# First batch of an attention-plus-MLP kernel as a stream of score and v rounds, wide relu in two batches, and free instruction order on three engines

## Chip, cores and metric

One NeuronCore of one Trainium2 chip. The metric is the device time of one execution in microseconds (us), lower is better. Times are medians over several runs.

TensorE is called PE below, VectorE DVE, ScalarE ACT, GpSimd POOL, SyncE SP. In the traces PE, ACT, DVE and POOL run side by side, each its own instructions, and one waits where it needs what another has made or still holds: in the kernel before PE waited 17.7 us for DVE between 8 and 52 us.

## The reference

Attention without softmax (relu squared in its place), then a two-layer MLP with relu squared.

```python
def _attn_ref(q, k, v):                       # q, k, v: (8, 12, 448, 64) fp32
    S = q.shape[2]
    scale = 1.0 / np.sqrt(q.shape[-1])
    scores = scale * np.matmul(q, k.transpose(0, 1, 3, 2))
    attn = np.maximum(scores, 0.0) ** 2 / S
    return np.matmul(attn, v).astype(np.float32)

def _moe_ref(x, w_in, w_out):                 # x: (3584, 768); w_in (768, 2048), w_out (2048, 768)
    h = x @ w_in
    r = np.maximum(h, 0.0)
    return ((r * r) @ w_out).astype(np.float32)

def reference(q, k, v, moe_w_in, moe_w_out):
    a = _attn_ref(q, k, v)                    # then (B, S, H * D) rows into the MLP
    ...
```

## The kernel before

A *unit* is four heads of one batch (three units a batch, 24 in all). A unit has seven *rounds*; a round computes one score tile `sp` (128 x 2 x 448 in PSUM) and turns it into `at` (fp16, SBUF) by relu squared. When a unit's seven tiles are there, `av` multiplies them by v into two PSUM tiles, which are evicted as `xt`. When three units of a batch are done, its *dense* work is queued: `hps` (x times w_in, relu squared into `g`) and, a batch later, `ops` (g times w_out, evicted as `osb` and stored). The dense matmuls are fed to PE in slices between score rounds. The first dense matmul can only come after the third unit; until then PE has transposes, scores and av alone, which kept it busy for 29.5 of the first 56.0 us.

```python
ctx.enter_context(tc.manual_schedule())       # all engines run in program order
...
s_p  = ...tile_pool(name="sps", bufs=2, space=PSUM)     # score tiles
mm_p = ...tile_pool(name="mmps", bufs=4, space=PSUM)    # av, hps, ops, transposes

def relu2(ps, dst, scale):                    # ps stays in PSUM through both
    nc.scalar.activation(out=dst, in_=ps, func=AF.Square, scale=scale)          # ACT
    nc.vector.scalar_tensor_tensor(                                             # DVE
        out=dst, in0=ps, scalar=0.0, in1=dst, op0=ALU.is_gt, op1=ALU.mult)

def soft(n, t, sp):
    at = at_p.tile([P, 2, S], FP16, name="at", tag="at")
    relu2(sp[:, :, 0:S], at, SK)
    ats[n, t] = at

def av(n):                                    # 28 matmuls, then two evictions
    ...
    for f in range(2):
        nc.scalar.activation(out=xts[b][:, 2 * u + f, :], in_=ap[f][:, 0:S],
                             func=AF.Copy, scale=CX)
...
for i in range(NB):                           # a burst is two rounds
    g = []
    for r in (2 * i, 2 * i + 1):
        n, t = divmod(r, TJ)
        g.append((n, t, scores(n, t)))        # PE
    if i in avs:
        av(avs[i])                            # PE, then ACT (xt)
    for a in g:
        soft(*a)                              # ACT, DVE
    if i in pushes:
        push_dense(pushes[i])
    upkeep(i)                                 # loads, casts, transposes of later units
    nxt = min([j for j in pushes if j > i] or [NB + 2])
    run_some(max(0.0, (queued - KEEP) / (nxt - i)))     # a slice of dense work
```

## Time and profile before

The kernel before takes 445.16 us (443.25 to 446.56, three runs). Its profiled run has a span of 441.0 us.

I cut the span at three marks of the trace: the first `hps` matmul (dense work can start), the first `ops` matmul (the second batch has been pushed) and the last `hps` matmul.

| stretch, profiled run before | us | what holds it |
|---|---|---|
| start to first hps | 56.0 | chains through ACT and DVE; PE busy 29.5 us |
| first hps to first ops | 45.0 | PE and DVE about even (busy 36.1 and 35.1 us) |
| first ops to last hps | 311.3 | PE (busy 307.2 us) |
| last hps to end | 28.7 | PE (ops; busy 23.8 us), then the last store |

First the page: busy time of each engine, and the row by slices of a fortieth of the span (11 us each) in tenths, with the granted PE clock.

```profile
PE 396.6 (90%) x3092; PEld 202.9 (46%) x3092; DVE 250.3 (57%) x309; ACT 261.8 (59%) x408; POOL 69.6 (16%) x92
...
PE   2565687799999999999999999999999999999995
...
PEclk9996599999999999999999999999999999999999
```

PE is full from the ninth slice on, and short of work in the first eight. In two of these its granted clock was also down, at 0.66 (33 to 44 us) and 0.50 (44 to 55 us).

The next lines are from the queries for one tile, with the start of the first and last instruction of each group: `hps` with the first and last quarter of w_in, and `ops` with the first quarter of w_out. The marks are 56.0, 101.0 and 412.3 us.

```profile
L166 PE MATMUL hps<-xt,w_0_90 x192: 352/353/363, 56.0 to 388.3; 128*128 128x448 f16 x192
...
L166 PE MATMUL hps<-xt,w_3_93 x192: 352/353/363, 88.5 to 412.3; 128*128 128x448 f16 x192
...
L194 PE MATMUL ops<-w_0_94,g x224: 326/326/337, 101.0 to 433.8; 128*128 128x384 f16 x112
```

The waits of PE from 8 to 52 us (who waited <- for whom: us in total, times, longest):

```profile
PE sp L240 <- DVE at L151: 17.7, 17, 3.0
...
```

And the waits of PE from 93 to 400 us, the whole list:

```profile
PE sp L240 <- DVE at L151: 4.5, 9, 0.6
```

PE waits for DVE to be done with a score tile, so that its PSUM can be written again: 17.7 us in 17 waits. In the long later part that is only 4.5 us.

One av burst of the first batch in the timeline (start, duration, engine, line, what; in brackets the engine's idle time before it and who ended it):

```profile
23.97 2.88 PE L263 MATMUL avt<-at,vs 64*64 64x448 f16 x28
...
26.91 0.98 ACT L269 ACTIVATE xt<-avt 128x448 f16<-128x448 f32 x2 [4.44 <-PE avt L263]
...
27.77 1.74 ACT L150 ACTIVATE at<-sp 128x896 f16<-128x896 f32 x2
...
28.73 1.09 DVE L151 SCALAR_TENSOR_TENSOR at<-sp,at 128x896 f16<-128x896 f32 x1 [5.13 <-ACT at L150]
```

ACT is idle for 4.44 us until av is finished, and DVE for 5.13 us.

The same spot in the later part, at the end of a unit:

```profile
120.06 0.57 PE L240 MATMUL sp<-qT,kT 64*64 64x448 f16 x8
...
120.47 1.49 PE L263 MATMUL avt<-at,vs 64*64 64x448 f16 x28
...
122.01 0.98 ACT L269 ACTIVATE xt<-avt 128x448 f16<-128x448 f32 x2 [2.30 <-PE avt L263]
...
122.88 1.74 ACT L150 ACTIVATE at<-sp 128x896 f16<-128x896 f32 x2
123.83 2.09 DVE L151 SCALAR_TENSOR_TENSOR at<-sp,at 128x896 f16<-128x896 f32 x2 [3.96 <-ACT at L150]
...
125.97 0.38 PE L240 MATMUL sp<-qT,kT 64*64 64x448 f16 x4 [0.49 <-DVE at L151]
```

### The profile page before, as it was taken

The numbers are of one execution on the slowest core, as the hardware profiler recorded it, in microseconds if no ns is written. First come the engines' busy times: TensorE is split into PE (matmuls) and PEld (weight loads), VectorE is DVE, ScalarE is ACT, GpSimd is POOL, SyncE is SP. The second block draws the span as 40 slices with busy tenths as digits, with TensorE's granted clock in tenths as the row PEclk, the third lists the DMA queues.
The fourth block names the chain that finished last, engine by engine and source line by source line (L and its number), as shares of the span: only waits on it lengthen the run. The fifth ranks groups of instructions, "written<-read, shape, count | busy, mean of one in ns | idle before, by whom it ended". The sixth has DMA issues, their size and how long they took to land.

```text
span 441.0 us, 7546 instructions
## 1 busy us (share of the span) xinstructions
PE 396.6 (90%) x3092; PEld 202.9 (46%) x3092; DVE 250.3 (57%) x309; ACT 261.8 (59%) x408; POOL 69.6 (16%) x92
## 2 busy tenths in 40 slices
PE   2565687799999999999999999999999999999995
PEld 1232243344445555444445455444445555555563
DVE  2754577776766574676586566486657555222100
ACT  4655478766676576587676665677667656433211
POOL 3710340131003100031103110310110000000000
PEclk9996599999999999999999999999999999999999
DMA  9699899667335764494647462595461111111122
GB/s 244 135 238 211 155 265 177 172 74 158 120 83 120 184 161 79 120 175 91 155 125 114 125 170 57 147 196 83 122 162 36 38 37 36 37 36 37 36 74 72
DMA packets 62883, 53.58 MB, mean 122 GB/s; under 512 B 35712, under 2 KB 59264, under 8 KB 62848
## 3 DMA queue, kind: packets, MB, share of 16 engines
q1 hardware_dynamic: 50944, 41.30, 37.3%
q0 software_dynamic: 11904, 11.80, 17.2%
q8 instruction: 24, 0.39, 0.4%
q14 instruction: 11, 0.09, 0.1%
HBM read 45.61 MB, written 11.01 MB: 128 GB/s over the span
## 4 chain that ended last, share of the span: by engine, by line
PE 76%; DVE 9%; ACT 8%; issue 4%; DMA 1%; SPq 0%; ACTq 0%; DVEq 0%
PE ops L194 31%; PE hps L166 27%; PE sp L240 9%; DVE at L151 9%; PE avt L263 8%; ACT at L150 4%; ACT xt L269 3%; PE tps L103 1%; DMA kf<-in_k_dram 1%; ACT kT L105 0%; DVE g L151 0%; DVE qT L105 0%; ACT ks L89 0%; ACT osb L201 0%; SPq L80 0%
## 5 line engine op out<-in xcount | busy, mean ns | idle before, releaser
L151 DVE SCALAR_TENSOR_TENSOR at<-sp,at 128x896 f16<-128x896 f32 x168 | 175.3, 1086 | 117.5 <-ACT at L150 117.3
L150 ACT ACTIVATE at<-sp 128x896 f16<-128x896 f32 x168 | 147.2, 925 | 27.9 <-PE sp L240 24.3
L194 PEld LDWEIGHTS <-g 128*128 128x128 f16 x896 | 85.3, 98 | 65.2 <-issue 8.9
L151 DVE SCALAR_TENSOR_TENSOR g<-hps,g 128x448 f16<-128x448 f32 x128 | 76.6, 618 | 41.0 <-ACT g L150 40.8
L240 PE MATMUL sp<-qT,kT 64*64 64x448 f16 x672 | 58.9, 392 | 34.0 <-DVE at L151 30.7
L150 ACT ACTIVATE g<-hps 128x448 f16<-128x448 f32 x128 | 68.9, 560 | 29.0 <-PE hps L166 28.5
L201 ACT ACTIVATE osb<-ops 128x384 f32<-128x384 f32 x56 | 27.7, 495 | 53.3 <-PE ops L194 45.6
L269 ACT ACTIVATE xt<-avt 128x448 f16<-128x448 f32 x48 | 23.5, 541 | 58.0 <-PE avt L263 58.0
L240 PEld LDWEIGHTS <-kT 64*64 64x64 f16 x672 | 16.9, 107 | 73.1 <-issue 69.7
L194 PE MATMUL ops<-w_2_96,g 128*128 128x384 f16 x224 | 47.0, 326 | 0.0
L194 PE MATMUL ops<-w_0_94,g 128*128 128x384 f16 x224 | 46.4, 326 | 0.0
L194 PE MATMUL ops<-w_3_97,g 128*128 128x384 f16 x224 | 46.3, 326 | 0.0
L194 PE MATMUL ops<-w_1_95,g 128*128 128x384 f16 x224 | 46.2, 327 | 0.0
L89 POOL CAST qs<-qf 128x896 f16<-128x896 f32 x23 | 21.5, 935 | 152.5 <-DMA qf<-in_q_dram 133.7
L166 PE MATMUL hps<-xt,w_1_91 128*128 128x448 f16 x192 | 40.9, 353 | 0.0
L166 PE MATMUL hps<-xt,w_2_92 128*128 128x448 f16 x192 | 40.7, 353 | 0.0
L166 PE MATMUL hps<-xt,w_3_93 128*128 128x448 f16 x192 | 40.5, 353 | 0.0
L263 PE MATMUL avt<-at,vs 64*64 64x448 f16 x672 | 39.7, 375 | 0.0
L166 PE MATMUL hps<-xt,w_0_90 128*128 128x448 f16 x192 | 39.7, 353 | 0.0
L114 POOL DMA_DIRECT2D vs<-in_v_dram x32 | 20.1, 636 | 94.8 <-PE hps L166 74.9
L263 PEld LDWEIGHTS <-vs 64*64 64x64 f16 x672 | 22.5, 114 | 12.5 <-issue 0.4
L166 PEld LDWEIGHTS <-w_1_91 128*128 128x128 f16 x192 | 18.1, 98 | 19.0 <-issue 4.0
(29 smaller groups left out, 113.0 us busy)
## 6 DMA issues: line engine op xcount, KB each, us to landing
qf<-in_q_dram SPq DMA_DIRECT2D x24, 448.0 KB, 4.5
kf<-in_k_dram SPq DMA_DIRECT2D x24, 448.0 KB, 5.0
out_dram<-osb SPq DMA_DIRECT2D x56, 192.0 KB, 2.7
vs<-in_v_dram POOLq DMA_DIRECT2D x32, 168.0 KB, 5.0
w_0_90<-in_moe_w_in_dram POOLq DMA_DIRECT2D x1, 768.0 KB, 7.4
w_1_91<-in_moe_w_in_dram POOLq DMA_DIRECT2D x1, 768.0 KB, 13.2
w_2_92<-in_moe_w_in_dram POOLq DMA_DIRECT2D x1, 768.0 KB, 17.2
w_3_93<-in_moe_w_in_dram POOLq DMA_DIRECT2D x1, 768.0 KB, 20.4
```

The source lines that it names most:

```text
L89: op(t.rearrange("p t (f d) -> p f t d", f=2), src.rearrange("p f (t d) -> p f t d", d=D))
L103: nc.tensor.transpose(ps[:, t * P:(t + 1) * P], src[:, t, :], ident)
L114: nc.gpsimd.dma_start(out=vst[b][64 * r:64 * r + 64, :, e, :], in_=src[h])
L150: nc.scalar.activation(out=dst, in_=ps, func=AF.Square, scale=scale)
L151: nc.vector.scalar_tensor_tensor(out=dst, in0=ps, scalar=0.0, in1=dst, op0=ALU.is_gt, op1=ALU.mult)
L166: nc.tensor.matmul(cell[0][:, 0:S], lhsT=w1[f // 4][:, m, (f % 4) * P:(f % 4 + 1) * P], rhs=xt[:, m, :], start=(m == 0), stop=(m == NM - 1))
L194: nc.tensor.matmul(cell[0][:, 0:HALF], lhsT=gt[f][:, tb * P:(tb + 1) * P], rhs=w2[f // 4][:, f % 4, hf * HALF:(hf + 1) * HALF], start=(f = ...
L201: nc.scalar.activation(out=cell[1][:, hf * HALF:(hf + 1) * HALF], in_=cell[0][:, 0:HALF], func=AF.Copy, scale=CO)
L240: nc.tensor.matmul(sp[64 * c:64 * c + 64, e, 0:S].rearrange("p (t c) -> p t c", t=TJ), lhsT=kT[r, t, 64 * e:64 * e + 64], rhs=qT[r, :, 64 ...
L263: nc.tensor.matmul(ap[f][64 * e:64 * e + 64, 0:S], lhsT=vs[r, u, e, t * D:(t + 1) * D], rhs=at[r, e, :], start=(t == 0), stop=(t == TJ - 1 ...
L269: nc.scalar.activation(out=xts[b][:, 2 * u + f, :], in_=ap[f][:, 0:S], func=AF.Copy, scale=CX)
```

## The change

Its intent: keep PE fed until dense work can start. The first batch becomes a stream: each round emits one score tile and, three rounds behind it, one v round, so that av no longer comes in bursts. For batches 0 and 1 the relu goes to SBUF as fp32 (ACT), which is meant to free PSUM without waiting for DVE, and the squaring reads SBUF (DVE, one tile of seven on POOL). Some small jobs move: the transposes' copies and, for these two batches, xt to DVE, and the q casts of all six units to ACT. Loads are issued in another order, and small DVE memsets that held some of them back are gone. And only PE and SP keep program order; ACT, DVE and POOL are ordered by the scheduler.

```diff
-    ctx.enter_context(tc.manual_schedule())
+    ctx.enter_context(tc.manual_schedule(engines={mybir.EngineType.PE, mybir.EngineType.SP}))
...
-    osb_p = ctx.enter_context(tc.tile_pool(name="osbp", bufs=3))
+    rel_p = ctx.enter_context(tc.tile_pool(name="widep", bufs=5))     # relu tiles and osb
...
+    def relu2_wide(ps, dst, scale, eng):
+        r = rel_p.tile([P, 2, S], FP32, name="rel", tag="wide")
+        nc.scalar.activation(out=r, in_=ps, func=AF.Relu, scale=scale)
+        eng.tensor_mul(dst, r, r)
...
     def soft(n, t, sp):
-        relu2(sp[:, :, 0:S], at, SK)
+        if n < NPE:                                   # NPE = 6 units, two batches
+            relu2_wide(sp[:, :, 0:S], at, SK, nc.gpsimd if t == 5 else nc.vector)
+        else:
+            relu2(sp[:, :, 0:S], at, SK)
...
-    def av(n):                                        # seven v rounds at once
+    def av(n, t):                                     # one v round; evicts after the seventh
...
+            if n < NPE:
+                nc.vector.tensor_scalar(
+                    out=dst, in0=ap[f][:, 0:S], scalar1=CX, scalar2=None, op0=ALU.mult)
+            else:
+                nc.scalar.activation(out=dst, in_=ap[f][:, 0:S], func=AF.Copy, scale=CX)
...
-    cast_qk(1, "q", pool)
     cast_qk(1, "k", pool)
+    cast_qk(1, "q", act)
...
+    early = {1: [(load_w1, 0)], 2: [(load_w1, 1)], 3: [(load_w1, 2)], 4: [(load_w1, 3)],
+             5: [(load_v, 1, (0, 1))], 7: [(load_v, 1, (2, 3))]}
...
                 if n == 0:
-                    cast_qk(2, "q", pool)
                     cast_qk(2, "k", pool)
+                    cast_qk(2, "q", act)
...
-    for i in range(NB):
+    for r in range(STREAM):                           # STREAM = 21 + LAG, LAG = 3
+        n, t = divmod(r, TJ)
+        sp = scores(n, t)
+        soft(n, t, sp)
+        if r >= LAG:
+            av(*divmod(r - LAG, TJ))
+        if n + 1 < NPE and t in (3, 5):
+            turn_pe(n + 1, "kq"[t // 4], dve)
+        if r % 2 == 0:
+            upkeep(r // 2)
+    push_dense(0)
+
+    for i in range(STREAM // 2, NB):                  # bursts as before, av ahead of soft
...
```

(The diff is cut; comments after code are mine.)

More of the change, by code (lines that the diff above doesn't have):

```diff
@@ L72, with load_qk @@
     vst: dict = {}
-    def load_qk(n, w, gate=None):
+    def load_qk(n, w, eng):
         b, u = divmod(n, NU)
         t = raw_p.tile([P, 2, TJ * D], FP32, name=w + "f", tag=w + "f")
-        if gate is not None:
-            gate.memset(t[:, 0, 0:1], 0.0)
         src = q if w == "q" else k
-        nc.sync.dma_start(
+        eng.dma_start(
             out=t,
@@ L183, in store @@
                     "(p t) d -> p t d", t=TJ)[:, t, :],
-                in_=osb[64 * i:64 * i + 64, :])
+                in_=osb[64 * i:64 * i + 64, 0:DM])
     def o_groups(pr, tb):
@@ L199, in run @@
                     if hf == 0:
-                        cell[1] = osb_p.tile([P, DM], FP32, name="osb", tag="osb")
+                        cell[1] = rel_p.tile([P, 2 * S], FP32, name="osb", tag="wide")
                     nc.scalar.activation(
@@ L247, in soft @@
         at = at_p.tile([P, 2, S], FP16, name="at", tag="at")
-        relu2(sp[:, :, 0:S], at, SK)
+        if n < NPE:
+            relu2_wide(sp[:, :, 0:S], at, SK, nc.gpsimd if t == 5 else nc.vector)
+        else:
+            relu2(sp[:, :, 0:S], at, SK)
         ats[n, t] = at
-    def av(n):
+    avs_open: dict = {}
+    def av(n, t):
         b, u = divmod(n, NU)
-        if u == 0:
+        if n == NU * b and t == 0:
             xts[b] = x_p.tile([P, NM, S], FP16, name="xt", tag="xt")
@@ L255, in av @@
         vs = vst[b]
-        ap = [mm_p.tile([P, 512], FP32, name="avt", tag="mm") for _ in range(2)]
-        for t in range(TJ):
-            at = ats.pop((n, t))
-            for e in range(2):
-                for c in range(2):
-                    f = c ^ e
-                    r = slice(64 * c, 64 * c + 64)
-                    nc.tensor.matmul(
-                        ap[f][64 * e:64 * e + 64, 0:S],
-                        lhsT=vs[r, u, e, t * D:(t + 1) * D],
-                        rhs=at[r, e, :],
-                        start=(t == 0), stop=(t == TJ - 1), skip_group_check=True)
@@ L268, in av @@
-        for f in range(2):
-            nc.scalar.activation(
-                out=xts[b][:, 2 * u + f, :], in_=ap[f][:, 0:S], func=AF.Copy, scale=CX)
-    pool, dve, act = nc.gpsimd.tensor_copy, nc.vector.tensor_copy, nc.scalar.copy
-    for n in range(3):
-        load_qk(n, "q")
-        load_qk(n, "k")
-    load_v(0, (0, 1))
+        if t == 0:
+            avs_open[n] = [mm_p.tile([P, 512], FP32, name="avt", tag="mm") for _ in range(2)]
+        ap = avs_open[n]
+        at = ats.pop((n, t))
@@ new lines, in av @@
+        for e in range(2):
+            for c in range(2):
+                f = c ^ e
+                r = slice(64 * c, 64 * c + 64)
+                nc.tensor.matmul(
+                    ap[f][64 * e:64 * e + 64, 0:S],
+                    lhsT=vs[r, u, e, t * D:(t + 1) * D],
+                    rhs=at[r, e, :],
+                    start=(t == 0), stop=(t == TJ - 1), skip_group_check=True)
+        if t < TJ - 1:
+            return
+        for f in range(2):
+            dst = xts[b][:, 2 * u + f, :]
+            if n < NPE:
[3 more added lines that the diff above has]
+                nc.scalar.activation(out=dst, in_=ap[f][:, 0:S], func=AF.Copy, scale=CX)
@@ L279 @@
+    pool, dve, act = nc.gpsimd.tensor_copy, nc.vector.tensor_copy, nc.scalar.copy
+    NPE = 6
+    load_qk(0, "k", nc.sync)
+    load_qk(0, "q", nc.scalar)
+    for n in (1, 2):
+        load_qk(n, "k", nc.sync)
+        load_qk(n, "q", nc.sync)
     ident = const_p.tile([P, P], FP16, name="ident", tag="ident")
     make_identity(nc, ident)
-    load_v(0, (2, 3))
-    cast_qk(0, "q", dve)
-    cast_qk(0, "k", act)
+    load_v(0, range(4))
+    cast_qk(0, "k", dve)
+    cast_qk(0, "q", act)
+    turn_pe(0, "k", dve)
@@ L284 @@
     turn_pe(0, "q", dve)
-    turn_pe(0, "k", act)
-    cast_qk(1, "q", pool)
     cast_qk(1, "k", pool)
+    cast_qk(1, "q", act)
     KEEP = 4000.0
-    NPE = 6
     ROUNDS = NUN * TJ
     NB = ROUNDS // 2
+    LAG = 3
+    STREAM = NU * TJ + LAG
     def av_burst(n):
         return (TJ * (n + 1) - 1) // 2 + 2
-    pushes = {av_burst(NU * b + 2): b for b in range(B)}
-    avs = {av_burst(n): n for n in range(NUN)}
+    pushes = {av_burst(NU * b + 2): b for b in range(1, B)}
+    avs = {av_burst(n): n for n in range(NU, NUN)}
@@ L300, in upkeep @@
+    early = {1: [(load_w1, 0)], 2: [(load_w1, 1)], 3: [(load_w1, 2)], 4: [(load_w1, 3)],
+             5: [(load_v, 1, (0, 1))], 7: [(load_v, 1, (2, 3))]}
     def upkeep(i):
+        for fn, *a in early.get(i, ()):
+            fn(*a)
         r0 = 2 * i
         for n in range(NUN):
+            b, u = divmod(n, NU)
             if r0 <= TJ * n < r0 + 2:
-                b, u = divmod(n, NU)
-                if 0 < n and n + 2 < NUN and n + 2 >= 3:
-                    load_qk(n + 2, "q", nc.vector if n + 2 < 6 else None)
-                    load_qk(n + 2, "k", nc.vector if n + 2 < 6 else None)
+                if 0 < n and n + 2 < NUN:
+                    for w in "kq":
+                        load_qk(n + 2, w, nc.sync)
@@ L309, in upkeep @@
                 if n == 0:
-                    cast_qk(2, "q", pool)
                     cast_qk(2, "k", pool)
-                    for z in range(4):
-                        load_w1(z)
-                    load_v(1, range(4))
+                    cast_qk(2, "q", act)
                 elif n == 3:
@@ L321, in upkeep @@
                 if 2 < n + 2 < NUN:
-                    cast_qk(n + 2, "q", pool)
                     cast_qk(n + 2, "k", pool)
-                if n + 1 < NUN:
-                    if n + 1 < NPE:
-                        turn_pe(n + 1, "q", dve)
-                        turn_pe(n + 1, "k", act)
+                    cast_qk(n + 2, "q", act if n + 2 < NPE else pool)
+                if STREAM <= r0 and n + 1 < NPE:
+                    for w in "kq":
+                        turn_pe(n + 1, w, dve)
                 if NPE <= n + 2 < NUN:
-                    turn_dma(n + 2, "q")
-                    turn_dma(n + 2, "k")
-    for i in range(NB):
+                    for w in "kq":
+                        turn_dma(n + 2, w)
+    for r in range(STREAM):
[10 more added lines that the diff above has]
+    for i in range(STREAM // 2, NB):
         g = []
@@ L337 @@
         if i in avs:
-            av(avs[i])
+            for t in range(TJ):
+                av(avs[i], t)
         for a in g:
@@ L347 @@
     for j in sorted(j for j in avs if j >= NB):
-        av(avs[j])
+        for t in range(TJ):
+            av(avs[j], t)
     for j in sorted(j for j in pushes if j >= NB):
```

## The prediction

> **What bounds the kernel now.** From about 93 us on it is TensorE. In the table of windows PE is busy 93.5 of 95 us (188 to 283 us), and the waits of PE between 93 and 400 us sum to only 4.5 us. Before that it is not: first dense matmul (hps) at 55.98 us, and from 54 to 93 us PE is busy 30.5 of 39 us. The waits of PE on the DVE half of relu-squared are 17.7 us up to 54 us and 8.5 us from 54 to 93. The timeline shows why. A score tile stays in PSUM through score matmuls (0.6 us), ACT Square (0.93) and DVE (1.09), with two buffers and two rounds per burst: a burst every 2.73 us (11.06, 13.79). Each of the three av bursts adds a hole: PE av 2.9 us, then xt on ACT, then scores again; DVE is idle about 5 us (23.6 to 28.7). The granted clock is 0.50 in much of 32 to 54 us.
>
> **What the change does.** (1) For batches 0 and 1 ACT writes Relu to SBUF and frees PSUM; chain per two rounds 0.6 + 0.93 = 1.6 us. The square costs DVE about what it cost before[...] 1.086 us measured for the PSUM form; no run shows the new form yet. (2) One round in seven goes to POOL[...]. (3) av is spread with a lag of three, removing the av holes. (4) DVE gets both turn copies (0.62 each) and xt (about 0.6 each); ACT gets a q cast (0.94).
>
> **Limit of the stream: DVE.** Per unit 6 x 1.09 + 2 x 0.62 + 2 x 0.6 = 9.0 us, ACT 7.5 us. Three units from 9.6 us would give dense work at about 38 us. [...]ACT may also be held by a q cast whose DMA is late (the second unit's loads landed at 9 to 11.3 us before). First hps: about 41 us, 14 to 15 us earlier.
>
> **Next ten bursts (before: 52 to 90.5 us).** DVE-bound again, estimated 11.7 us a unit plus contention against 12.8 before: gain 0 to 5 us, I take 1.
>
> **On the critical path.** All of this lies ahead of the TensorE-bound stretch, so it goes through to the end. DMA is the second limit: reads needed before dense work are about 13.6 MB, near 36 us at the rate of the saturated stretch, so the start cannot move much below 38 us. Later batches: order of ACT, DVE and POOL now chosen by the scheduler, at most 1% either way.
>
> **Predicted: 430 us, 421 to 440.** Faster by over 2% 0.76, within 2% 0.21, slower 0.03.
>
> **What would show it.** First hps at 38 to 45 us; score waits released by ACT, not DVE; DVE over 80% busy from 10 to 40 us; DVE squares near 1.09 us, longer where POOL overlaps; clock at 0.50 for less time; after the second batch, the same 47.5 us per batch.
>
> **What would make it wrong.** Strong DVE/POOL blocking (squares over 1.4 us on average, first hps past 47 us); weight loads hoisted by the scheduler that delay q and k; ACT blocked early by a cast; a worse order in the steady part.

Three passages are cut from this text, as what they argued rested on no run or trace of this case. The 1.09 us of a wide square: the 1.086 us of the old form, measured in the kernel before, gives the same term. An allowance of 1 us a unit for squares that POOL's work holds up (the "contention" of its paragraph on the ten bursts): estimate, and not shown by the trace of before, where POOL's 46 casts all took 0.93 to 0.94 us. The forecast of about 41 us for the first hps came from the 38 us above it and three times this allowance. The third is an estimate of a POOL square's time; the six of the kernel after took 1.95 us on average. The 430 us are 445.16 less about 14 us at the first hps and 1 us in the ten bursts.

Of the terms, 0.62 is the copy of qT on DVE in the kernel before (617 ns), 0.94 its cast of k on ACT (937 ns), and 0.6 for xt on DVE an estimate, near the 618 ns that DVE took there for `g`, which has the size of xt and also comes from PSUM. Run after the forecast, the kernel after took 0.610 us for xt.

## More of the kernel before

The instructions that stand in line on an engine are called its queue here.

Note the place of `av` and `soft` in a burst: in program order ACT meets the eviction of `av` first and the Square of the two fresh score tiles after it.

## The result, and the profile after

The kernel after takes 429.34 us (427.43 to 429.66, four runs), the one before 444.64 us in the same rounds. The ratio is 0.9646, with a 95% interval of 0.9606 to 0.9686. A ratio here is the mean time of one kernel's fast runs over that of the other's fast runs of the same rounds, so it is not quite the ratio of the medians. Executions over 1.5% slower than the fastest of the same kernel are left out of the means.

The gain in time is the predicted one, 15.3 us against 15.2. Its place is not.

| stretch, profiled runs | before | after | gain | the prediction's term |
|---|---|---|---|---|
| start to first hps | 56.0 | 50.7 | 5.3 | 14 to 15 |
| first hps to first ops | 45.0 | 40.6 | 4.4 | about 1 (its ten bursts are nearly this stretch) |
| first ops to last hps | 311.3 | 305.7 | 5.6 | none ("at most 1% either way", entered as 0) |
| last hps to end | 28.7 | 28.6 | 0.1 | none |
| span | 441.0 | 425.6 | 15.4 | |

The marks after:

```profile
L170 PE MATMUL hps<-xt,w_0_90 x192: 349/352/363, 50.7 to 373.0; 128*128 128x448 f16 x192
...
L170 PE MATMUL hps<-xt,w_3_93 x192: 352/352/363, 77.6 to 397.0; 128*128 128x448 f16 x192
...
L198 PE MATMUL ops<-w_0_94,g x224: 326/326/336, 91.3 to 418.5; 128*128 128x384 f16 x112
```

The same lines of the page (a slice is 10.6 us here):

```profile
PE 389.6 (92%) x3092; PEld 198.4 (47%) x3092; DVE 261.8 (62%) x315; ACT 255.5 (60%) x395; POOL 79.3 (19%) x93
...
PE   2456688799999999999999999999999999999995
...
PEclk9988899999999999999999999999999999999999
```

The PE row is hardly better in the first eight slices. It is not the row of a kernel whose start was cured. The waits of PE from 8 to 52 us:

```profile
PE sp L244 <- ACT rel L155: 8.1, 7, 6.7
PE tps L101 <- DVE xt L284: 5.0, 2, 2.9
PE avt L274 <- DVE at L156: 3.1, 3, 1.3
PE hps L170 <- DVE xt L284: 1.9, 1, 1.9
...
```

Score tiles are now released by ACT, as intended, but new waits have come: 8.1 us for ACT, 6.7 of them at once, and 5.0 and 1.9 us for `mm` PSUM that DVE had not emptied of av. From 93 to 400 us the list of PE's waits is now empty.

The 6.7 us are at the very start:

```profile
8.11 0.96 PE L244 MATMUL sp<-qT,kT 64*64 64x448 f16 x8 [0.72 <-DVE qT L103]
...
9.43 0.94 ACT L87 CAST qs<-qf 128x896 f16<-128x896 f32 x1 [3.15 <-DMA qf<-in_q_dram]
...
13.94 0.94 ACT L87 CAST qs<-qf 128x896 f16<-128x896 f32 x1 [3.57 <-DMA qf<-in_q_dram]
14.78 1.72 ACT L155 ACTIVATE rel<-sp 128x896 f32<-128x896 f32 x2
...
15.74 0.59 PE L244 MATMUL sp<-qT,kT 64*64 64x448 f16 x4 [6.67 <-ACT rel L155]
```

Two score tiles are ready before 9.1 us. But the q casts of the second and third unit stand ahead of the first Relu in ACT's queue (the program puts the first of them there, the scheduler the other as well), and those wait for loads. In the trace ACT stands 3.57 us in front of the second cast with Relus ready behind it. The first Relu starts at 14.78 us; before, the first Square started at 8.97.

The later part, at the same spot as above:

```profile
109.56 0.57 PE L244 MATMUL sp<-qT,kT 64*64 64x448 f16 x8
...
109.96 1.49 PE L274 MATMUL avt<-at,vs 64*64 64x448 f16 x28
110.00 1.73 ACT L148 ACTIVATE at<-sp 128x896 f16<-128x896 f32 x2 [0.72 <-PE sp L244]
...
110.94 2.09 DVE L149 SCALAR_TENSOR_TENSOR at<-sp,at 128x896 f16<-128x896 f32 x2 [1.58 <-ACT at L148]
...
111.61 0.99 ACT L287 ACTIVATE xt<-avt 128x448 f16<-128x448 f32 x2
```

Here is the part that the prediction had not seen. The program text of the bursts still says av first, then relu squared. With ACT free, the scheduler has swapped them: the Squares run *beside* av, and xt comes after. DVE's idle time falls from 3.96 to 1.58 us, and PE never waits for PSUM.

Finally the new squares on DVE, from the page's groups:

```profile
L156 DVE TENSOR_TENSOR at<-rel 128x896 f16<-128x896 f32 x36 | 43.7, 1253 | 11.6 <-ACT rel L155 11.5
```

Their mean is 1253 ns. Undisturbed ones take 1.08 us (those with no POOL work near them), seven of the 36 take 1.7 to 2.5 us, six of them where a POOL cast or square ran beside them and one where POOL was issuing loads. 36 x (1253 - 1080) ns = 6.2 us, on average about 1 us for each of the six units. (In all ten profiled runs with wide squares, none of the 139 squares without any POOL work beside them took over 1.2 us, and 91 of the 160 beside a cast or square did.) The prediction charged 1 us a unit for this, the author's estimate. For this kernel that term was right.

### The profile page after: what moved, and what is told of

Read it like the earlier page. It is cut to its first block, busy times and chain, and to the rows that moved or that the text cites. A ratio compares the mean times of both kernels' runs of the same rounds, so it can differ in the third digit from the quotient of the medians.

```text
span 425.6 us, 7547 instructions
## 1 busy us (share of the span) xinstructions
PE 389.6 (92%) x3092; PEld 198.4 (47%) x3092; DVE 261.8 (62%) x315; ACT 255.5 (60%) x395; POOL 79.3 (19%) x93
## 4 chain that ended last, share of the span: by engine, by line
PE 82%; DVE 10%; DMA 3%; ACT 2%; issue 2%; SPq 0%; ACTq 0%; DVEq 0%
PE ops L198 35%; PE hps L170 32%; PE sp L244 8%; DVE at L156 7%; PE avt L274 6%; DMA qf<-in_q_dram 3%; ACT rel L155 1%; DVE g L149 1%; PE tps L101 1%; DVE xt L284 1%; SPq L78 0%; DVE qT L103 0%; DVE at L149 0%; DVE kT L103 0%; ACT qs L87 0%
## 5 line engine op out<-in xcount | busy, mean ns | idle before, releaser
L149 DVE SCALAR_TENSOR_TENSOR at<-sp,at 128x896 f16<-128x896 f32 x126 | 131.6, 1086 | 66.0 <-ACT at L148 65.8
L148 ACT ACTIVATE at<-sp 128x896 f16<-128x896 f32 x126 | 108.8, 915 | 40.9 <-PE sp L244 40.5
L149 DVE SCALAR_TENSOR_TENSOR g<-hps,g 128x448 f16<-128x448 f32 x128 | 77.5, 620 | 53.0 <-ACT g L148 52.3
L244 PE MATMUL sp<-qT,kT 64*64 64x448 f16 x672 | 53.5, 379 | 13.1 <-ACT rel L155 8.1
L87 POOL CAST ks<-kf 128x896 f16<-128x896 f32 x23 | 23.1, 1003 | 197.0 <-DMA kf<-in_k_dram 185.8
L156 DVE TENSOR_TENSOR at<-rel 128x896 f16<-128x896 f32 x36 | 43.7, 1253 | 11.6 <-ACT rel L155 11.5
L274 PE MATMUL avt<-at,vs 64*64 64x448 f16 x672 | 41.7, 364 | 3.1 <-DVE at L156 3.1
L155 ACT ACTIVATE rel<-sp 128x896 f32<-128x896 f32 x42 | 35.8, 920 | 12.8 <-PE sp L244 12.8
L244 PEld LDWEIGHTS <-kT 64*64 64x64 f16 x672 | 15.4, 107 | 45.8 <-issue 40.3
L274 PEld LDWEIGHTS <-vs 64*64 64x64 f16 x672 | 21.3, 110 | 15.4 <-issue 5.5
```

Source lines behind the costliest of these rows:

```text
L87: op(t.rearrange("p t (f d) -> p f t d", f=2), src.rearrange("p f (t d) -> p f t d", d=D))
L149: nc.vector.scalar_tensor_tensor(out=dst, in0=ps, scalar=0.0, in1=dst, op0=ALU.is_gt, op1=ALU.mult)
L155: nc.scalar.activation(out=r, in_=ps, func=AF.Relu, scale=scale)
L156: eng.tensor_mul(dst, r, r)
L244: nc.tensor.matmul(sp[64 * c:64 * c + 64, e, 0:S].rearrange("p (t c) -> p t c", t=TJ), lhsT=kT[r, t, 64 * e:64 * e + 64], rhs=qT[r, :, 64 ...
L274: nc.tensor.matmul(ap[f][64 * e:64 * e + 64, 0:S], lhsT=vs[r, u, e, t * D:(t + 1) * D], rhs=at[r, e, :], start=(t == 0), stop=(t == TJ - 1 ...
```

## The experiments

My theory after the result, in three parts:

- **A (order).** The gain behind the first hps comes from ACT squaring the scores ahead of evicting xt, not from the stream or the wide form. Rival R: the first batches leave the later ones in a better state.
- **B (lost start).** The stream's own gain was cut by ACT's late start (casts ahead of the first Relu) and by PE waiting for PSUM that DVE empties late. Rival: loads, or DVE with POOL, bound it anyway.
- **C (parts).** What the wide form, the POOL squares and the spread av are worth each.

All twelve experiments gave correct results. They ran in four groups, each with its own runs of the kernel before, so between groups compare ratios. The time of a profiled run differs from the median of its kernel by up to 3 us (before: 442.76 us, against medians of 444.64 to 445.85), so stretches read from one profile carry that; the stretch from first ops to last hps is an exception and repeats within 0.1 us.

| run | median us | ratio to before (95%) | first Relu or Square | start to first hps | first hps to first ops | first ops to last hps |
|---|---|---|---|---|---|---|
| before | 444.64 | 1 | 8.97 | 56.0 | 45.0 | 311.3 |
| after | 429.34 | 0.9646 (0.9606 to 0.9686) | 14.78 | 50.7 | 40.6 | 305.7 |
| b_free | 433.36 | 0.9727 (0.9698 to 0.9757) | 8.79 | 58.6 | 39.6 | 305.7 |
| b_soft | 427.41 | 0.9599 (0.9574 to 0.9624) | 9.36 | 51.2 | 39.6 | 305.7 |
| a_man | 434.95 | 0.9775 (0.9751 to 0.9799) | 10.35 | 49.2 | 44.0 | 311.3 |
| a_man_soft | 427.10 | 0.9613 (0.9586 to 0.9641) | 10.19 | 49.1 | 43.5 | 305.7 |
| a_qpool | 427.10 | 0.9578 (0.9550 to 0.9607) | 8.86 | 47.0 | 41.7 | 305.7 |
| a_allvec | 430.64 | 0.9661 (0.9634 to 0.9689) | 15.07 | 49.5 | 44.7 | 305.7 |
| a_narrow | 431.29 | 0.9661 (0.9634 to 0.9687) | 14.97 | 53.5 | 41.7 | 305.7 |
| a_burst | 427.85 | 0.9604 (0.9571 to 0.9636) | 14.89 | 50.6 | 40.6 | 305.8 |
| c_qx | 425.45 | 0.9539 (0.9510 to 0.9568) | 9.04 | 41.6 | 49.2 | 305.8 |
| c_qx3 | 423.46 | 0.9501 (0.9470 to 0.9532) | 8.91 | 42.0 | 43.2 | 305.7 |
| c_n3 | 422.75 | 0.9500 (0.9475 to 0.9524) | 8.81 | 45.0 | 41.6 | 305.8 |
| c_qxv | 421.96 | 0.9476 (0.9446 to 0.9505) | 9.17 | 43.2 | 42.7 | 305.7 |

The last column takes only two values, 311.3 and 305.7 (or 305.8). It is 311.3 in exactly the two kernels in which ACT meets xt ahead of the Squares. The columns before it carry a second difference, the granted clock: ahead of the first hps it was at 0.50 for 20.5 us in before, 10.2 in after and b_soft, 13.7 in a_man and a_qpool, 3.4 in c_qx. No run separates what this is worth.

### b_free: the kernel before, free order on ACT, DVE and POOL

```diff
-    ctx.enter_context(tc.manual_schedule())
+    ctx.enter_context(tc.manual_schedule(engines={mybir.EngineType.PE, mybir.EngineType.SP}))
```

> Kernel before, with nothing changed but the fixed order kept for TensorE and SP alone. Theory A (about 6 of the 15 us come in the TensorE-bound part, because the free order lets ACT square the scores before it evicts xt): 4 to 7 us faster than before, ratio 0.984 to 0.991; waits of PE on DVE between 93 and 400 us fall from 4.5 us to under 1; first hps within 3 us of 56. Rival R (the later part gained from what the first batches left behind, not from the order): ratio 0.997 to 1.003, PE waits stay near 4.5 us.

Measured: 433.36 us, ratio 0.9727; no PE wait from 93 to 400 us; first hps at 58.6 us. The later part gains the full 5.6 us, and the stretch from first hps to first ops 5.4, so theory A holds for the later part and rival R falls. The gain is larger than expected (12 us in the medians, 8.4 in the profiled runs), because I had read the order's effect only off the later part. The start itself became slower: with free order PE waited 8.1 us once on a score tile.

### b_soft: the kernel before, full program order, two statements swapped

```diff
-        if i in avs:
-            av(avs[i])
         for a in g:
             soft(*a)
+        if i in avs:
+            av(avs[i])
```

> Kernel before in full fixed order, but in each burst the relu-squared is written ahead of av, so that ACT's order is scores first, then xt. TensorE's order is the same. Theory A: this one swap gives the same later gain, ratio 0.980 to 0.991, PE waits between 93 and 400 us under 1 us. Rival R: ratio 0.997 to 1.003.

Measured: 427.41 us, ratio 0.9599. This is below the expected range; the swap gains in all three stretches (4.8, 5.4 and 5.6 us). PE's order is untouched, since `soft` gives PE nothing to do. In the timeline:

```profile
109.10 0.57 PE L240 MATMUL sp<-qT,kT 64*64 64x448 f16 x8
...
109.50 1.49 PE L263 MATMUL avt<-at,vs 64*64 64x448 f16 x28
109.53 1.73 ACT L150 ACTIVATE at<-sp 128x896 f16<-128x896 f32 x2 [0.78 <-PE sp L240]
110.48 2.09 DVE L151 SCALAR_TENSOR_TENSOR at<-sp,at 128x896 f16<-128x896 f32 x2 [1.58 <-ACT at L150]
...
111.14 0.99 ACT L269 ACTIVATE xt<-avt 128x448 f16<-128x448 f32 x2
```

These are the lines of after, with the same idle times. The swap alone, without stream, wide form or free order, is as fast as the whole change (0.9599 against 0.9646; the intervals overlap). The "hole of the av burst" in the first batch was largely the same thing, ACT standing at xt with two score tiles ready: at the first burst ACT's idle time before xt falls from 4.44 to 1.51 us, and DVE's before its next square from 5.13 to 1.52.

### a_man: the kernel after, all engines in program order

```diff
-    ctx.enter_context(tc.manual_schedule(engines={mybir.EngineType.PE, mybir.EngineType.SP}))
+    ctx.enter_context(tc.manual_schedule())
```

> Kernel after with every engine in fixed program order. Theory A: PE waits in the TensorE-bound part return (4 us or more), time 433 to 437 us; first Relu near 10.4 us as only one of the two casts stands ahead of it. Rival R: within 1 us of after.

Measured: 434.95 us, first Relu at 10.35 us, first ops to last hps back at 311.3, and PE waits of 4.0 us from 93 to 400 us:

```profile
PE sp L244 <- DVE at L149: 4.0, 8, 0.6
```

As theory A expected. So the stream and its parts alone are worth 10.6 us (445.57 less 434.95 of the same rounds), and the free order brings the rest. The two are not additive: the order alone, in b_soft, was worth 18 us, as it also shortened the start that the stream was built for (by 4.8 us).

### a_man_soft: the same with the swap in the bursts

```diff
+        for a in g:
+            soft(*a)
         if i in avs:
             for t in range(TJ):
                 av(avs[i], t)
-        for a in g:
-            soft(*a)
```

> Kernel after in full fixed order (that run: 435 us, 355.3 us from first to last hps), with only the swap of relu-squared ahead of av in the bursts behind the stream. Theory A (what the free order gave is this one swap): first hps near 49, 345 to 347.5 us from first to last hps, no PE wait from 93 to 400 us, time 425 to 429.5 us. Rival (the scheduler's other reorderings do it): more than 350 us from first to last hps, time above 431 us.

Measured: 427.10 us, first hps at 49.1, no PE wait from 93 to 400 us, and 305.7 in the last column: the swap is what the free order gave the later part. From first to last hps it takes 349.2 us in the profiled run, above the expected 345 to 347.5: between first hps and first ops it stays at 43.5 us, where after has 40.6. Whether some other reordering by the scheduler helped after there is not shown: in this run the clock was at 0.50 from 81.2 to 84.6 us, inside this stretch, where after had it full, and PE was busy 36.4 us of the stretch against 34.8 for as many matmuls. That leaves 1.3 of the 2.9 us. (This profiled run, 428.72 us, was also near the slowest of its six.)

### a_qpool: the late start taken away

```diff
-    cast_qk(1, "q", act)
+    cast_qk(1, "q", pool)
...
-                    cast_qk(2, "q", act)
+                    cast_qk(2, "q", pool)
```

> Kernel after, the q casts of the second and third unit on POOL instead of ACT. Theory B (the stream started 6 us late, at 14.8 us, because ACT's queue had these two casts, waiting for their loads, ahead of the first Relu): first Relu at about 9 us, first hps 4 to 6 us earlier than 50.7, time 423 to 426 us. Rival (the stream is bound by loads or by DVE with POOL contention, and the early wait is absorbed later): first Relu at 9 us but first hps moves less than 2 us, time 427.5 to 430.

Measured: first Relu at 8.86 us, first hps at 47.0, time 427.10 us. Six us earlier at the start became 3.7 at first hps and 2 to 3 at the end: less than theory B asked for, more than the rival allowed. PE's 4.8 us of waits for DVE's evictions are no new limit, since after had 5.0. What is new lies right behind the early start: PE stood at av until a load of v had landed (1.31 us, up to 13.80 us), with the next unit's transposes behind it, and ACT was idle for 3.61 us before its fifth Relu at 15.81 us. So loads took part of the gain, as the rival had it. (The profiled run, 424.83 us, was the fastest of its six.)

### c_qx: in addition xt evicted by ACT in the first two batches

```diff
# on a_qpool
-            if n < NPE:
+            if n < 0:
                 nc.vector.tensor_scalar(out=dst, ...)
             else:
                 nc.scalar.activation(out=dst, ...)
```

> Kernel after with the q casts of the second and third unit on POOL and, for batches 0 and 1, xt evicted by ACT instead of DVE. Theory B2 (with the late start gone, the stream is held by PE waiting for PSUM that DVE has not yet emptied of av, 4.8 us in the run with the q casts moved): those waits fall under 1.5 us, first hps at 43 to 45.5 us instead of 47.0, time 422 to 425.5 us. Rival (loads bind: the stream cannot go faster, waits move to the transposes of late units or to v): first hps stays at 46 to 48 us.

Measured: first hps at 41.6 us, 5.4 earlier still and better than expected. PE's waits for the eviction fall to 0.2 us. (Whether the waits or the 1.1 us of DVE work a unit mattered more, this edit can't tell: it takes away both.) So about 41 us, the prediction's figure for first hps, is reached only with xt taken off DVE. DVE was then busy 28.4 of the 30 us from 10 to 40 (22.1 in after), so DVE is the limit here, as the prediction had said for its own assignment of work. Yet the time is only 425.45 us. In the profiled run, the slowest of its five (426.99 us), of the 9.1 us won at first hps over after, 8.6 are lost again up to first ops (49.2 against 40.6 us). The timeline shows where:

```profile
71.47 2.14 PE L274 MATMUL avt<-at,vs 64*64 64x448 f16 x20
...
75.11 0.93 POOL L87 CAST ks<-kf 128x896 f16<-128x896 f32 x1 [5.50 <-DMA kf<-in_k_dram]
...
76.22 0.93 POOL L87 CAST qs<-qf 128x896 f16<-128x896 f32 x1 [0.18 <-DMA qf<-in_q_dram]
77.12 1.68 POOL L156 TENSOR_TENSOR at<-rel 128x896 f16<-128x896 f32 x1
...
78.85 0.96 PE L274 MATMUL avt<-at,vs 64*64 64x448 f16 x8 [5.24 <-POOL at L156]
...
79.74 2.80 PE L170 MATMUL hps<-xt,w 128*128 128x448 f16 x7
```

One POOL square stands in POOL's queue behind two casts that wait for loads, and the av on PE needs it. PE stands 5.24 us. And its clock is down; the table of windows, with start and end, busy time of PE, PEld, DVE, ACT and POOL, the granted clock, DMA share and GB/s:

```profile
72.00:76.00 4.00, 1.61 (x20) 0.74 (x13) 1.72 (x2) 0.70 (x1) 0.89 (x1) 0.50 0.78 235
76.00:80.00 4.00, 1.15 (x9) 0.32 (x9) 0.00 (x0) 0.15 (x1) 2.61 (x3) 0.50 0.64 117
80.00:84.00 4.00, 4.00 (x12) 1.67 (x11) 0.73 (x2) 1.91 (x4) 0.73 (x1) 0.50 0.71 229
```

From 80 to 84 us PE is fully busy and gets 12 matmuls done, at half clock. In finer windows the clock is 0.70 from 71.0 to 71.5 us, so it fell just before the stand, and full from 85.0 us on.

### c_qx3: POOL squares in the first batch only

```diff
-            relu2_wide(sp[:, :, 0:S], at, SK, nc.gpsimd if t == 5 else nc.vector)
+            relu2_wide(sp[:, :, 0:S], at, SK, nc.gpsimd if t == 5 and n < NU else nc.vector)
```

> As the run with q casts on POOL and xt on ACT, but POOL squares only in the stream (first batch), DVE does all of them in the second. Theory E (that run won 9 us at the start and gave it back because one POOL square stood in POOL's queue behind q and k casts that waited for late loads; PE then stood 5.2 us and its clock fell to half): the 5.2 us wait and the half clock near 72 to 85 us go, first hps stays at 41 to 42.5, time 416 to 421 us. Rival (loads as such bind the second batch, the POOL square only showed it): PE waits move to transposes or scores, time 423 to 426 us.

Measured: the 5.24 us wait is gone, and first hps to first ops is 43.2 us instead of 49.2. The clock of the same windows:

```profile
72.00:76.00 4.00, 1.42 (x28) 0.92 (x31) 4.00 (x6) 1.76 (x3) 0.94 (x1) 1.00 0.59 217
76.00:80.00 4.00, 4.00 (x37) 1.86 (x33) 2.69 (x4) 2.62 (x6) 0.94 (x1) 1.00 0.69 122
80.00:84.00 4.00, 4.00 (x33) 1.80 (x33) 3.31 (x5) 3.24 (x6) 1.02 (x2) 1.00 0.70 222
```

33 matmuls in the window that had 12 (the 12 were all hps; of the 33, 16 are the shorter score matmuls). Theory E of the expectation (the gain was given back at one POOL square) holds for the mechanism. The time, 423.46 us, misses its range of 416 to 421 by 2.5 us and lies in the rival's range, and the interval overlaps that of c_qx; the profiled run (421.32 us) was the fastest of its five, that of c_qx the slowest, so the 6 us between their stretches overstate the gain. PE's waits did move to scores, as the rival said, but in its trace the longest is DVE's doing:

```profile
43.08 4.95 DVE L156 TENSOR_TENSOR at<-rel 128x896 f16<-128x896 f32 x2
...
48.63 0.57 PE L244 MATMUL sp<-qT,kT 64*64 64x448 f16 x8 [2.83 <-DVE qT L103]
```

Two squares took 4.95 us (2.2 undisturbed) while POOL ran three casts beside them, and the copy of qT that PE waited for stood behind them. The clock was also at 0.50 from 49.3 to 52.7 us. What each is worth in the 43.2 us, against 40.6 in after, I did not separate.

### c_n3: in addition the old relu squared in the second batch

```diff
# on c_qx
-        if n < NPE:
+        if n < NU:
             relu2_wide(...)
```

> As the last, and in the second batch the old relu-squared from PSUM instead of the wide form. If the wide form is worth something there, 2 to 5 us slower than the last run; if, as in the swap run (39.6 us from first hps to first ops with the old form, 40.6 in after with the wide), it is worth nothing, within 1.5 us of it: 416 to 422 us.

Measured: 422.75 us, ratio 0.9500 against 0.9501 in the same rounds. The time is 0.7 us above the range but within the 1.5 us. In the second batch the wide form is worth nothing that five rounds show. Its place is mixed: first hps came 3.0 us later than in c_qx3 (the stream's last three rounds belong to the second batch), and 1.6 us of this were regained up to first ops.

### c_qxv: no POOL squares at all

```diff
# on c_qx
-            relu2_wide(sp[:, :, 0:S], at, SK, nc.gpsimd if t == 5 else nc.vector)
+            relu2_wide(sp[:, :, 0:S], at, SK, nc.vector)
```

> As the first of these, no POOL square at all. By the ablation on after (no POOL square: 1.3 us later) first hps 1 to 3 us later than with POOL squares in the stream, time 417 to 423 us.

Measured: 421.96 us, ratio 0.9476, the best: 5.2% below before, and by the two ratios to before (0.9476 over 0.9646, different rounds) 1.8% below after. First hps is 1.2 us later than in c_qx3, as expected, but the end is not later. Against c_qx3 the intervals overlap: POOL squares cost or gain nothing that five rounds show.

### a_allvec: the kernel after without POOL squares

The same edit on after.

> Kernel after with all wide squares on DVE, none on POOL. Theory C (POOL's squares cost DVE part of what they save: hit squares took 1.7 to 2.5 us instead of 1.08): six squares more on DVE, 6.5 us, less 3 us of blocking, spread over two batches: first hps 1 to 3 us later than 50.7, time 429.5 to 432 us. If blocking were nil: first hps 3 us or more later and 432 to 436. Mean wide square falls from 1.253 to 1.10-1.18 us, as the k casts remain on POOL.

Measured: 430.64 us, inside the range, so POOL squares are worth about 1 us there and the intervals overlap. But first hps came at 49.5 us, 1.2 *earlier*, where I expected 1 to 3 later; the loss is between first hps and first ops (44.7 against 40.6). The mean wide square fell to 1.153 us.

### a_narrow: the kernel after with the old relu squared throughout

```diff
-        if n < NPE:
+        if n < 0:
             relu2_wide(...)
```

> Kernel after with the old relu-squared (Square, then DVE from PSUM) in all batches; stream, lag and casts as in after. If the early release of PSUM is what makes the stream fast, first hps is 3 us or more later than 50.7 and the time 432 to 437 us. Rival, from the run of before with only the order swapped (427.4 us without any wide form): the wide form is worth nothing once the order is right, time 427 to 431 us.

Measured: first hps at 53.5 us, 2.8 later; 431.29 us. It lies between the two expectations. The wide form with its POOL squares is worth 2 to 3 us in the stream, no more; the ratios (0.9661 and 0.9646) do not separate.

### a_burst: the kernel after with av in bursts in the stream

```diff
-        if r >= LAG:
-            av(*divmod(r - LAG, TJ))
+        if r >= LAG and (r - LAG) % TJ == TJ - 1:
+            for z in range(TJ):
+                av((r - LAG) // TJ, z)
```

> Kernel after with the av matmuls of a unit of the stream in one burst, at the place of its last one. If spreading av is worth what the change meant it for, the holes of 2 to 3 us come back three times: first hps 3 us or more later, time 432 to 436 us. Rival (the hole of before came from ACT standing at xt ahead of the next Square, not from the burst): first hps within 1.5 us of 50.7, time 427.5 to 431 us.

Measured: 427.85 us, first hps at 50.6 (after: 50.7). Spreading av, the idea that gave the change its name, is worth nothing that can be seen. With b_soft, the rival holds: the hole came from ACT's order. (PE's waits changed kind: the 5.0 us for evictions are gone, one of 5.4 us for a qT copy has come. In c_qx, where less stands in the stream's way, bursts were not tried.)

## Why the prediction was right, and where it was not

- **The time.** 430 us predicted, 429.34 measured. Right by luck: the first term was some 9 us too large, and the two behind it 9 us too small together.
- **"First hps: about 41 us, 14 to 15 us earlier."** This is the step that failed: it came at 50.7. What it left out was order and buffers. ACT's queue had two q casts ahead of the first Relu (first Relu at 14.78 us instead of about 9; moving them gave 3.7 us at first hps), and DVE emptied av's PSUM so late that PE waited 6.9 us for it (5.0 + 1.9; moving xt to ACT gave 5.4 us). The first had been named among what would make the prediction wrong, but with no size in the estimate. The sum of work (9.0 us of DVE a unit, plus 1 us of blocking) was too small as well: c_qx needed 41.6 us although xt, 1.2 of the 9.0 us, was off DVE. There 20 squares ran before the first hps, not 18, since the lag puts three more rounds ahead of the last v round, and squares beside POOL's work took 6.2 us more than undisturbed, not 3.
- **"From about 93 us on it is TensorE"; "Later batches: ... at most 1% either way."** The second failed step. PE was 98.7% busy there, and yet 5.6 us of 311.3 (1.8%) could be had, and 4.5 of these were in the list of waits that the prediction quoted as small. They all had one cause that was visible in the program: ACT met xt ahead of the Squares. Both directions were tested: giving before the other order removes the 5.6 us (b_soft, b_free), giving after the old one brings them back (a_man).
- **"removing the av holes."** The holes were real, the cause was not. a_burst keeps the bursts and loses nothing; b_soft keeps the bursts and the old relu and loses nothing against after.
- **Blocking of DVE by POOL, 1 us a unit.** Right for after, as a mean: 6.2 us over six units (in c_qx it was 6.2 us in the first three). "DVE squares near 1.09 us, longer where POOL overlaps" came out as well: the undisturbed time, 1.08 us, is within 1% of the 1.09 us in the prediction's sum, and of the 1.086 us measured for the old form, and six squares beside POOL's casts or squares took 1.7 to 2.5 us.
- **The ten bursts.** A gain of 0 to 5 us was allowed and 1 taken; the nearest stretch gave 4.4, again mostly by order: b_soft gained 5.4 there without any wide form.
- **"score waits released by ACT, not DVE"; "clock at 0.50 for less time".** Both right (ahead of the first hps, at 0.50 for 10.2 us in after and 20.5 in before).
- **"DVE over 80% busy from 10 to 40 us".** Wrong: 22.1 of 30 us, 73%. For 5.7 of the missing 7.9 us DVE waited for the late first Relu.
- **"The start cannot move much below 38 us" for DMA.** 13.6 MB in 36 us are 378 GB/s; in the trace of before the HBM reads from 20 to 40 us come to 394 GB/s, an estimate from the packets (those of q0 count twice, as the program loads fp32 into fp16 tiles there). The limit was not put to the test: no run's first hps came before 41.6 us.
- **"after the second batch, the same 47.5 us per batch."** Wrong, for the reason above.

Three things stay open: what brings after's second batch from 43.5 to 40.6 us (a_man_soft against after), beyond the clock; how the limits on the second batch in c_qx3 and c_qxv (DVE's squares beside POOL's casts, the clock) divide; and how much of the gains ahead of the first hps is the clock.

## What to carry to other kernels

Where an engine takes its instructions in order, as ACT did here (3.57 us in front of a cast, with Relus ready behind it), ask of every instruction that waits what ready work stands behind it: swapping two statements in the old kernel was worth 18 us here, the rebuilt first batch without the swap 10.6. When a change alters both structure and instruction order, run the order alone on the old kernel before crediting the structure. And a small list of waits on the bottleneck engine is still a list of gains if all its entries have one cause; an early gain, on the other hand, has to be followed to the end, because the next queue (here one POOL square behind two casts) may give it all back.

## What else the traces show

- A square on POOL (896 elements a partition, the same tile as both inputs) took 1.68 us where DVE was idle (the line at 77.12 us in c_qx), 1.68 to 2.52 us in the kernel after.
- Where squares of DVE met work of POOL, either could be slow: squares that met POOL's casts or squares took up to 2.5 us instead of 1.08, and POOL's k casts up to 1.6 us instead of 0.93 in the kernel after. Whether POOL's load issues do so as well is open: one square of after (1.81 us, at 23.77 us) was slow with nothing but load issues on POOL beside it, and so in all ten runs with wide squares were 4 of 58 such squares, which is too little to decide.
- The clock came back late: in c_qx PE worked without pause from 78.85 us, and the clock was full only from 85.0 us, about 6 us later. Why is not shown. Each single half-clock stretch in the first 100 us of these traces lasts 3.4, 6.8, 10.2 or 13.7 us.
